# One PSUM pool for attention and experts, in a fused kernel on one Trainium2 core

## The chip, the core and the metric

The kernel runs on one core of one Trainium2 chip. The metric is the device time of one execution in microseconds (us); lower is better. A time "of the runs" is the median of several executions; the profile is of one execution more, with a time of its own.

The engines go by their profile names: PE (matrix multiply, with PEld for its weight loads), ACT, DVE and POOL for element-wise work, and SP, which here only issues transfers. PE writes its results to PSUM, an accumulator memory of eight banks; each bank holds 512 fp32 numbers on each of 128 partitions. ACT and DVE read them from there.

## The reference

Two stages. The first is a gated attention unit without a softmax, the second sends each of its 22528 output rows through a dense two-layer network and, in addition, through the one expert network (of eight) that its largest logit picks, weighted by that expert's softmax probability.

```python
# u, v: [8, 2816, 256]   z: [8, 2816, 64]   F = 512, E = 8
scores = (1.0 / S) * np.matmul(z, z.transpose(0, 2, 1))
x = (u * np.matmul(np.maximum(scores, 0.0) ** 2, v)).reshape(22528, 256)

y = np.maximum(x @ w1_dense, 0.0) @ w2_dense
e = np.argmax(x @ w_gate, axis=1)             # gate_w = softmax(x @ w_gate)[e]
y += gate_w[:, None] * (np.maximum(x @ w1[e], 0.0) @ w2[e])      # row by row
```

## The kernel before

The whole program is unrolled in Python. The order of PE, ACT, DVE and SP is the order in which the code calls them (a manual schedule); a framework then gives each tile its place and adds every semaphore wait. A tile that is taken anew from a pool waits until all users of the tile that held its place are done.

**Attention.** The loop over `groups` works a batch off in blocks of 128 queries. `scores` makes score tiles `s` on PE, `relu` turns them into the squared matrix `A` in two steps on ACT, DVE or POOL, `av` multiplies them with `v` into `o` (L603), and `gate_x` (L630) multiplies `o` by `u`, which gives two blocks of rows of `x`. `s`, `o`, and the small routing products (`lg` for the logits, `pre` for counts) all lie in four pairs of PSUM banks. A pair is asked for with `take_pair`, given back with `give_pair`, and a tile on it is made with `banks(x, name)`, which takes a new tile of the tag `b0` to `b3` from the pool `ps` (one place for each tag). Which pair is taken next follows times that the code estimates as it writes the program.

**Routing.** For each group `q` of row blocks (eleven blocks, with smaller ones at the end) `logits`, `route_a`, `route_pre` and `route_b` find each row's expert and its place in a table in DRAM, and `scatter` writes the rows there (L749). The last two groups are routed in the expert phase (`late_routing`, `late_places`), and their `lg` and `pre` tiles come from the expert phase's PSUM tiles: for the last but one from the `y` tiles, for the last from the `s` tiles (function `small`).

**Experts.** After the loop the attention's pool is closed, and two pools are opened on its banks:

```python
attention.close()
late["s"] = pool("psS", 3, space=bass.MemoryType.PSUM)     # three tiles of two banks
late["y"] = pool("psY", 2, space=bass.MemoryType.PSUM)     # two tiles of one bank
```

Then `slot(s)` is called for each tile of 256 rows, 90 of them. For tile `s` a slot makes the dense hidden layer (`up` with `w1d`), the second half of tile `s - 2`, the expert's hidden layer of tile `s` (`up` with the expert's weights), and the first half of tile `s - 1`. Between, it fetches rows some slots ahead over SP (`fetch`) and copies the weights of the next tile's expert into a ring with DVE (`expert`, L960).

- `up` writes eight matmuls into one `h_ps` tile of two banks (L973), and ACT applies Relu into the ring of hidden tiles (L976).
- `half(s, j)` does 128 rows: four matmuls for the dense part into `y[:, 0, :]`, four for the expert's into `y[:, 1, :]`, both in one `yy` tile of one bank (L982); ACT copies the dense part to SBUF (L999); DVE multiplies the expert's part by the gate and adds the copy (L1000); POOL writes the rows to the output by an indirect DMA (L1002). For some halves POOL also runs a small copy (`pause`, L987).

So PE's order in the expert phase is: 8 matmuls of `h_ps`, 8 of `yy`, 8 of `h_ps`, 8 of `yy`, and so on. The `yy` tiles alternate between the two places of `psY`, the `h_ps` tiles go round the three of `psS`.

Of the kernel before, what the change touches and what calls it, by code (L numbers as in the profile page):

```python
# [8 lines left out]
F32 = mybir.dt.float32  # L9
# [6 lines left out]
P = 128  # L16
# [3 lines left out]
def kernel(  # L20
# [13 lines left out]
    B, S, D = u.shape  # L34
# [11 lines left out]
    nQ = len(sizes)  # L46
# [21 lines left out]
    def pool(name, bufs, **kw):  # L68
        return ctx.enter_context(tc.tile_pool(name=name, bufs=bufs, **kw))
# [6 lines left out]
    tt = pool("tt", 1)  # L76
    mx = pool("mx", 6)
    NS = 4
    attention = ExitStack()
    ps = attention.enter_context(tc.tile_pool(name="ps", bufs=1, space=bass.MemoryType.PSUM))  # L80
    late = {}

    def banks(x, name, shape=(P, 2, 4 * P), dt=F32):

        return ps.tile(list(shape), dt, name=name, tag=f"b{x}")
# [61 lines left out]
    def load_u(g, gate=False):  # L147
        ut = aw.tile([P, 2, D], F32, name="ut", bufs=3)
        if gate:
            nc.vector.memset(ut[:, 0, 0:1], 0.0)  # L150
        b, i = divmod(g, nK)
        nc.sync.dma_start(out=ut[:], in_=uf[:, b, i:i + 2, :])
        issue(0.6)
        ut_of[g] = ut[:]
# [131 lines left out]
    pairs = [(0.0, x) for x in range(NS - 2)]  # L286
# [49 lines left out]
    def until(cond):  # L336

        while cond() is None:
            pick = best()
            assert pick is not None  # L340
            now[0] = max(now[0], pick[0][0])
            give(pick)
        now[0] = max(now[0], cond())
        run(now[0])
# [38 lines left out]
    def take_pair():  # L383
        return pairs.pop(0)[1]
# [82 lines left out]
    def block(n, k, c):  # L467

        w = groups[n][2]
        for a in far[n]:  # L470
            _, j0, wj = groups[a]
            if j0 <= k < j0 + wj:
                x = c * wj + k - j0
                return turned_to(a, n, w)[:, x * P:(x + 1) * P]
        return A[n][:, k, c * P:(c + 1) * P]

    def far_steps(a):

        _, j0, wj = groups[a]

        def step(ns):
            n = ns[0]
            i0, w = groups[n][1], sum(groups[m][2] for m in ns)
            if n == a + 2:
                open_group(a + 1)
                open_group(n)
            nc.sync.dma_start_transpose(
                out=turned_to(a, n, w).rearrange("p (x c) -> p x c", c=P),
                in_=A[a][:, i0:i0 + w, :].rearrange("p k c -> p (k c)"))
            issue(0.18 * w * wj, read_at.get(a - 1, 0.0) if n == a + 2 else 0.0)  # L490
            read_at[a] = sync[0] + 3.5
            for m in ns:
                for j in range(wj):
                    key_at[m, j0 + j] = sync[0] + 3.0

        ns = [[n] for n in range(a + 2, min(a + 6, len(groups))) if a in far[n]]
        if len(ns) == 4:
            ns[2:] = [ns[2] + ns[3]]
        elif groups[a][2] == 4:
            ns = ns[1:] + ns[:1]  # L500
        return [(a, lambda m=m: step(m), m[-1]) for m in ns]
# [5 lines left out]
    def fill(n, force=False):  # L507

        if jobs and jobs[0][0] <= now[0] and room(1):
            jobs.pop(0)[1]()  # L510
            return True
        m = ahead(n)
        busy = sum(1 for op in todo if op[0] in (1, 4))
        if m is not None and room(1) and busy <= (4 if n < 2 else 2):
            scores(m, left[m].pop(0))
            return True
        return False
# [9 lines left out]
    def v_at(n, k):  # L527

        return 3.3 + 2.6 * (4 * k // nK) if n == 0 else 0.0

    def need(n, k):

        while max(key_at.get((n, k), 9e9), v_at(n, k)) > now[0]:
            if fill(n):
                continue
            pick = best()
            ts = [t for t, _ in pairs if t > now[0]]
            ts += [max(key_at[n, k], v_at(n, k))] if (n, k) in key_at else []
            assert pick is not None or ts
            if pick is not None and (not ts or pick[0][0] <= min(ts)):  # L540
                now[0] = max(now[0], pick[0][0])
                give(pick)
            else:
                now[0] = min(ts)
        run(now[0])
# [31 lines left out]
    def av(n, i, between):  # L577
        b, i0, w = groups[n]
        if i == i0:
            turning.extend(far_steps(n))  # L580
        keep[0] = 0
        if n == 0 and i == i0:

            fill(n)
            need(n, 0)
        until(lambda: pairs[0][0] if pairs else None)
        ox = take_pair()
        o = banks(ox, "o")
        for p in range(2):
            rest = list(range(nK))  # L590
            for x in range(nK):
                k = rest[0]
                if i == i0 and p == 0:

                    k = min(rest, key=lambda k: (max(key_at.get((n, k), 9e9), v_at(n, k)), k))
                    need(n, k)
                rest.remove(k)
                if n == 0 and i == i0 and p == 0 and x in (12, 14, 16):
                    load_u(2 * (x - 12) // 2, gate=True)
                for h in range(2):  # L600
                    r = slice(h * dq, (h + 1) * dq)
                    j = p ^ h
                    nc.tensor.matmul(out=o[:, j, 0:D], lhsT=block(n, k, i + j - i0)[r],  # L603
                                     rhs=v_of[b][r, k, :], start=(p == 0 and x == 0),
                                     stop=(p == 1 and x == nK - 1))
                pe(0.1092)
                keep[0] = 2 - p if x >= nK - 12 else 0
                if x % 2 == 1 and x < nK - 1:
                    fill(n)
                if x in (3, 10, 17)[1 - p:] and turning and sync[0] <= now[0] + 0.5:  # L610
                    t = can_turn(turning[0][2], turning[0][0])
                    if t is not None and t <= now[0]:
                        turning.pop(0)[1]()
            if p == 0:
                swap_rows(n)
                between()

        def done(t):
            give_pair(t + 0.1, ox)

        g = b * nK + i
        offer(now[0] + 0.2, 0, {"dve": (0.63, lambda eng: gate_x(g, o))}, done)
        keep[0] = 0
# [21 lines left out]
    def small(q, name, shape):  # L645
        if q < nQ - 2:
            return banks(bank_of[q], name, shape)
        tag = "y" if q == nQ - 2 else "s"
        return late[tag].tile(list(shape), F32, name=name, tag=tag)

    def logits(q):
        n = sizes[q]
# [311 lines left out]
    def up(xT, ws):  # L964

        m = xT.shape[1]
        h_ps = late["s"].tile([P, 4, 2, P], F32, name="h_ps", tag="s")
        n = m // len(ws)
        for i, w1 in enumerate(ws):
            hs = slice(i * n, (i + 1) * n)  # L970
            for f in range(4):
                for c in range(2):
                    nc.tensor.matmul(out=h_ps[:, f, hs, :], lhsT=w1(c, f), rhs=xT[:, hs, c, :],  # L973
                                     start=(c == 0), stop=(c == 1))
        h = take("h")
        nc.scalar.activation(h[:, :, 0:m * P], h_ps[:, :, 0:m, :].rearrange("p f h t -> p f (h t)"),  # L976
                             AF.Relu)
        return h
# [12 lines left out]
    def half(s, j):  # L991

        hd, he, we, me, ids = pend[s]
        we = we[j % len(we)]
        yd, ys = take("yd"), take("ys")
        y = late["y"].tile([P, 2, D], F32, name="yy", tag="y")
        down(y, 0, hd, lambda f: w2d[:, f, :], j)
        down(y, 1, he, lambda f: we[:, 2 * F + f * D:2 * F + (f + 1) * D], j)
        nc.scalar.copy(yd, y[:, 0, :])  # L999
        nc.vector.scalar_tensor_tensor(out=ys, in0=y[:, 1, :], scalar=me[:, j, 0:1],  # L1000
                                       in1=yd, op0=ALU.mult, op1=ALU.add)
        ins = nc.gpsimd.indirect_dma_start(  # L1002
            out=out, out_offset=bass.IndirectOffsetOnAxis(ap=ids[j], axis=0),
            in_=ys, in_offset=None, bounds_check=N - 1, oob_is_err=False)
        nodep(ins, ["out"], "out")
        last_row[0] = ins
        if j == 0 and s < NT1:
            pause(ys)
# [180 lines left out]
    while jobs:  # L1189
        jobs.pop(0)[1]()  # L1190
        run(9e9)
    attention.close()
    late["s"] = pool("psS", 3, space=bass.MemoryType.PSUM)
    late["y"] = pool("psY", 2, space=bass.MemoryType.PSUM)
    for s in range(NT - MAYBE + 2):
        assert s + AHEAD < NT1 or not waiting
        slot(s, NT - MAYBE)
# [45 lines left out]
```

## Time and profile before

| what | value |
|---|---|
| median of 3 runs | 905.04 us (904.14 to 910.75) |
| profiled execution, its own time | 909.34 us |
| its span | 907.6 us |
| PE busy | 862.3 us, 95% of the span |
| ACT busy | 697.8 us, 77% |
| DVE busy | 667.2 us, 74% |
| POOL busy | 468.1 us, 52% |
| granted PE clock | 0.998 of full speed |
| first matmul into `h_ps` | 552.0 us |
| first and last matmul into `yy` | 554.8 us and 899.1 us |

In the groups of instructions, `L999 ACT COPY ring<-yy` is the ACT copy at line 999, which reads the tile `yy` and writes a tile named `ring`; then come the shapes and the count, the busy time and the mean of one in ns, and after the second bar how long the engine had been idle right before these instructions and what ended most of it. In a timeline each row has start, duration, engine, line, operation, and in brackets the idle time before it. A row of windows has a stretch, its length, and the busy time of PE, PEld, DVE, ACT and POOL with the count of instructions, then the granted PE clock, the DMA share and the rate. A row of waits has who waited for whom, the total in us, how often, and the longest. The ends of matmuls are modelled: PE starts one of the small ones every 0.109 us, and the profile gives each 0.272 us.

### The profile page before, as it was taken

The page shows a single profiled execution, that of the slowest core. Times are in us where ns is not written, and L with a number is a line of the kernel's source. Part 1 is how long each engine was busy: PE and PEld are TensorE (multiplying, and loading weights), DVE is VectorE, ACT ScalarE, POOL GpSimd, SP SyncE. Part 2 cuts the span into 40 slices and gives each one's busy share as a digit, 9 for nine tenths or more (in the row PEclk, how much of TensorE's full clock was granted, in tenths as well). Part 3 has the DMA queues.
Part 4 walks back from the last instruction along what each step waited for, and adds up shares of the span by engine and source line. Part 5 has one row for each costly group of instructions (what it writes and reads, how often), then busy time and mean ns, then how long its engine had stood idle before and what let it go on. Part 6 is the DMA issues. An engine that isn't in the chain of part 4 may idle for free.

```text
span 907.6 us, 30096 instructions
## 1 busy us (share of the span) xinstructions
PE 862.3 (95%) x12178; PEld 754.2 (83%) x12178; DVE 667.2 (74%) x1268; ACT 697.8 (77%) x871; POOL 468.1 (52%) x510
## 2 busy tenths in 40 slices
PE   7999999999999999999999999988989898999996
PEld 5898798898898888889889877877878787888885
DVE  7998898898889889889889976456644444546554
ACT  8988798888889879879879964666666666776664
POOL 8202343343353444343334354777778777877454
PEclk9999999999999999999999999999999999999999
DMA  9999999999999999999998874645434453443332
GB/s 179 156 192 165 184 193 169 201 196 180 213 182 186 199 178 187 199 175 195 205 178 153 163 126 94 129 113 116 112 101 115 108 109 107 109 103 100 88 89 83
DMA packets 288238, 136.80 MB, mean 151 GB/s; under 512 B 258526, under 2 KB 265950, under 8 KB 287200
## 3 DMA queue, kind: packets, MB, share of 16 engines
q1 hardware_dynamic: 263552, 79.40, 52.5%
q0 software_dynamic: 24544, 55.44, 26.3%
q8 instruction: 96, 1.57, 0.7%
q14 instruction: 46, 0.38, 0.1%
HBM read 61.54 MB, written 37.03 MB: 109 GB/s over the span
## 4 chain that ended last, share of the span: by engine, by line
PE 70%; POOL 10%; issue 9%; DVE 4%; ACT 3%; DMA 2%; POOLq 0%; another core or an unknown queue 0%; DVEq 0%; SPq 0%; ACTq 0%
PE o L603 41%; PE yy L982 9%; PE h_ps L973 9%; PE s L405 9%; POOL out_dram L1002 7%; POOL zr L987 1%; DMA out_dram<-ring,ix 1%; ACT A L433 1%; ACT r L420 1%; DVE r L422 1%; PE lg L659 1%; POOL A L435 1%; DMA wall<-A 1%; DVE ring L1000 1%; ACT ring L999 1%
## 5 line engine op out<-in xcount | busy, mean ns | idle before, releaser
L603 PE MATMUL o<-vb,A 64*128 64x256 bf16 x7184 | 458.9, 269 | 3.1 <-POOL A L435 1.3
L603 PEld LDWEIGHTS <-A 64*128 64x128 bf16 x7184 | 378.8, 94 | 44.2 <-issue 3.3
L749 POOL DMA_INDIRECT xs<-pays,pi x176 | 191.9, 1090 | 283.0 <-DVE pi L747 232.1
L420 ACT ACTIVATE r<-s 128x1024 f32<-128x1024 f32 (+1 forms) x252 | 247.1, 1011 | 44.4 <-PE s L405 42.1
L976 ACT ACTIVATE ring<-h_ps 128x1024 bf16<-128x1024 f32 x180 | 184.6, 1027 | 96.1 <-PE h_ps L973 61.1
L433 ACT ACTIVATE A<-r 128x1024 bf16<-128x1024 f32 (+1 forms) x238 | 242.1, 1047 | 7.3 <-DMA wall<-A 4.6
L1000 DVE SCALAR_TENSOR_TENSOR ring<-yy,me,ring 128x256 f32<-128x256 f32 x179 | 85.6, 481 | 154.3 <-ACT ring L999 82.9
L435 DVE TENSOR_TENSOR A<-r 128x1024 bf16<-128x1024 f32 x151 | 182.9, 1221 | 4.0 <-ACT r L420 3.0
L422 DVE TENSOR_SCALAR r<-s 128x1024 f32<-128x1024 f32 (+1 forms) x145 | 175.0, 1214 | 8.7 <-PE s L405 6.0
L1002 POOL DMA_INDIRECT out_dram<-ring,me x140 | 147.1, 1051 | 66.2 <-DVE ring L1000 31.2
L982 PEld LDWEIGHTS <-ring 128*128 128x128 bf16 x1432 | 138.9, 98 | 44.6 <-issue 28.9
L405 PE MATMUL s<-zT 64*128 64x512 bf16 (+1 forms) x874 | 145.1, 355 | 1.8 <-ACT zT L199 0.6
L982 PE MATMUL yy<-w2d,ring 128*128 128x256 bf16 x716 | 107.3, 272 | 22.8 <-DVE ring L1000 20.2
L982 PE MATMUL yy<-ring 128*128 128x256 bf16 x716 | 107.6, 273 | 0.3 <-issue 0.3
L973 PE MATMUL h_ps<-ring 128*128 128x256 bf16 (+1 forms) x872 | 94.6, 254 | 1.2
L973 PE MATMUL h_ps<-ring,w1d 128*128 128x256 bf16 x720 | 93.1, 272 | 2.3 <-DVE pays L630 1.6
L999 ACT COPY ring<-yy 128x256 f32<-128x256 f32 x179 | 67.7, 378 | 29.2 <-PE yy L982 18.1
L960 DVE COPY ring<-wall 128x2048 bf16 x109 | 81.8, 765 | 10.2 <-issue 6.2
L630 DVE TENSOR_TENSOR pays<-o,ut 128x512 bf16<-128x512 f32 x88 | 60.2, 685 | 30.6 <-PE o L603 29.0
L973 PEld LDWEIGHTS <-ring 128*128 128x128 bf16 x872 | 73.0, 98 | 11.7 <-DVE ring L960 2.7
L973 PEld LDWEIGHTS <-w1d 128*128 128x128 bf16 x720 | 69.9, 98 | 11.0 <-issue 3.0
L405 PEld LDWEIGHTS <-zT 64*128 64x128 bf16 x874 | 54.2, 94 | 17.5 <-issue 6.7
(122 smaller groups left out, 426.6 us busy)
## 6 DMA issues: line engine op xcount, KB each, us to landing
ut<-in_u_dram SPq DMA_DIRECT2D x88, 256.0 KB
vb<-in_v_dram POOLq DMA_DIRECT2D x7, 1408.0 KB
wall<-in_moe_w_dram POOLq DMA_DIRECT2D x16, 256.0 KB
xs<-pays,pi POOLq DMA_INDIRECT x176
zr<-in_z_dram POOLq DMA_DIRECT2D x7, 352.0 KB
out_dram<-ring,me POOLq DMA_INDIRECT x140
ring<-xs SPq DMA_TRANSPOSE x114
xT<-pays SPq DMA_TRANSPOSE x88
```

The lines of the kernel that those rows point to most:

```text
L405: nc.tensor.matmul(out=s[:, h, y * c:(y + 1) * c], lhsT=zT[r, k + h, :], rhs=zT[r, i0:i0 + w, :], start=True, stop=True)
L420: nc.scalar.activation(r[:, :, :c], s[:, :, :c], AF.Relu, scale=1.0 / S)
L422: nc.vector.tensor_scalar(out=r[:, :, :c], in0=s[:, :, :c], scalar1=1.0 / S, scalar2=0.0, op0=ALU.mult, op1=ALU.max)
L433: nc.scalar.activation(a, r, AF.Square)
L435: (nc.gpsimd if eng == "pool" else nc.vector).tensor_mul(a, r, r)
L603: nc.tensor.matmul(out=o[:, j, 0:D], lhsT=block(n, k, i + j - i0)[r], rhs=v_of[b][r, k, :], start=(p == 0 and x == 0), stop=(p == 1 and x ...
L749: ins = nc.gpsimd.indirect_dma_start(out=xs, out_offset=bass.IndirectOffsetOnAxis(ap=pi[:], axis=0), in_=pays[:, g % (2 * G), 0:ROW].bitca ...
L973: nc.tensor.matmul(out=h_ps[:, f, hs, :], lhsT=w1(c, f), rhs=xT[:, hs, c, :], start=(c == 0), stop=(c == 1))
L976: nc.scalar.activation(h[:, :, 0:m * P], h_ps[:, :, 0:m, :].rearrange("p f h t -> p f (h t)"), AF.Relu)
L982: nc.tensor.matmul(out=y[:, k, :], lhsT=h[:, f, j * P:(j + 1) * P], rhs=w2(f), start=(f == 0), stop=(f == 3))
L1000: nc.vector.scalar_tensor_tensor(out=ys, in0=y[:, 1, :], scalar=me[:, j, 0:1], in1=yd, op0=ALU.mult, op1=ALU.add)
L1002: ins = nc.gpsimd.indirect_dma_start(out=out, out_offset=bass.IndirectOffsetOnAxis(ap=ids[j], axis=0), in_=ys, in_offset=None, bounds_chec ...
```

## The change

The pool `ps` stays open for the whole kernel, and the pools `psS` and `psY` are gone. After the attention loop, the pair that was not used by the last `o` and is first free becomes one tile named `yy`; its two banks serve the halves in turn, as slices `yy[:, 0, :]` and `yy[:, 1, :]`. The two other such pairs and then the pair of the last `o` serve `h_ps` in turn; for each `h_ps` a new tile is taken with `banks`. The `lg` and `pre` of the last but one group are slices of the `yy` tile, those of the last group new tiles on the `h_ps` pairs. No instruction is added or taken out on any engine.

```diff
     NS = 4
-    attention = ExitStack()
-    ps = attention.enter_context(tc.tile_pool(name="ps", bufs=1, space=bass.MemoryType.PSUM))
+    ps = pool("ps", 1, space=bass.MemoryType.PSUM)
+    last_o = []
...
         ox = take_pair()
         o = banks(ox, "o")
+        last_o[:] = [ox]
...
     def small(q, name, shape):
         if q < nQ - 2:
             return banks(bank_of[q], name, shape)
-        tag = "y" if q == nQ - 2 else "s"
-        return late[tag].tile(list(shape), F32, name=name, tag=tag)
+        if q == nQ - 1:
+            return next_h(name, shape)
+        a, b = shape[1:]
+        return next_y()[:, 0:a * b].rearrange("p (a b) -> p a b", b=b)
+
+    def next_h(name, shape):
+        late["h"].append(late["h"].pop(0))
+        return banks(late["h"][-1], name, shape)
+
+    def next_y():
+        late["y"].append(late["y"].pop(0))
+        return late["y"][-1]
...
-        h_ps = late["s"].tile([P, 4, 2, P], F32, name="h_ps", tag="s")
+        h_ps = next_h("h_ps", (P, 4, 2, P))
...
-        y = late["y"].tile([P, 2, D], F32, name="yy", tag="y")
+        y = next_y().rearrange("p (k d) -> p k d", d=D)
...
-    attention.close()
-    late["s"] = pool("psS", 3, space=bass.MemoryType.PSUM)
-    late["y"] = pool("psY", 2, space=bass.MemoryType.PSUM)
+    other = [x for _, x in pairs if x not in last_o]
+    assert len(other) == NS - 1
+    yy = banks(other.pop(0), "yy")
+    late["y"] = [yy[:, x, :] for x in range(2)]
+    late["h"] = other + last_o
```

## The prediction

> **What bounds the kernel now.** I read the page's head first, then the groups of the expert phase, one stretch of windows over that phase, the waits, and three pieces of the timeline: a quiet piece, a stall, and the change of phase.
>
> ```profile
> span 907.6 us, 30096 instructions
> PE 862.3 (95%) x12178; PEld 754.2 (83%) x12178; DVE 667.2 (74%) x1268; ACT 697.8 (77%) x871; POOL 468.1 (52%) x510
> PE 70%; POOL 10%; issue 9%; DVE 4%; ACT 3%; DMA 2%; POOLq 0%; another core or an unknown queue 0%; DVEq 0%; SPq 0%; ACTq 0%
> L999 ACT COPY ring<-yy 128x256 f32<-128x256 f32 x179 | 67.7, 378 | 29.2 <-PE yy L982 18.1
> L1000 DVE SCALAR_TENSOR_TENSOR ring<-yy,me,ring 128x256 f32<-128x256 f32 x179 | 85.6, 481 | 154.3 <-ACT ring L999 82.9
> ...
> L982 PE MATMUL yy<-w2d,ring x716: 269/272/273, 554.8 to 898.7; 128*128 128x256 bf16 x179
> ...
> 559.20:894.00 334.80, 309.80 (x2917) 270.42 (x2916) 173.85 (x366) 220.77 (x346) 240.87 (x277) 1.00 0.46 106
> ...
> PE yy L982 <- DVE ring L1000: 20.2, 22, 2.4
> ```
>
> PE is the bound, and the chain that ended last runs over PE for 70% of the span. The expert phase runs from the first yy matmul at 554.8 to the last at 898.7 and a few microseconds more. There are 716/4 = 179 "halves" of 128 tokens in it. In each, PE makes 8 matmuls into h_ps and 8 into one yy tile; ACT copies the dense part of yy (L999, 378 ns); DVE combines the two parts (L1000, 481 ns). PE is busy 309.8 of 334.8 us between 559.2 and 894.0, so there is little idle time for a new wait to hide in. PE already waits for the combining, 20.2 us in all, but only 22 times in 179: with two yy tiles it waits for the half before the last.
>
> The quiet piece is the one to learn from:
>
> ```profile
> 700.22 0.60 PE L982 MATMUL yy<-w2d,ring 128*128 128x256 bf16 x4
> 700.65 0.60 PE L982 MATMUL yy<-ring 128*128 128x256 bf16 x4
> 701.09 1.04 PE L973 MATMUL h_ps<-ring 128*128 128x256 bf16 x8
> 701.34 0.37 ACT L999 COPY ring<-yy 128x256 f32<-128x256 f32 x1
> 701.79 0.48 DVE L1000 SCALAR_TENSOR_TENSOR ring<-yy,me,ring 128x256 f32<-128x256 f32 x1 [1.26 <-issue]
> 701.96 0.60 PE L982 MATMUL yy<-w2d,ring 128*128 128x256 bf16 x4
> 702.16 1.02 ACT L976 ACTIVATE ring<-h_ps 128x1024 bf16<-128x1024 f32 x1 [0.46 <-issue]
> 702.50 0.73 DVE L960 COPY ring<-wall 128x2048 bf16 x1 [0.22 <-issue]
> 703.21 0.37 ACT L999 COPY ring<-yy 128x256 f32<-128x256 f32 x1
> 703.62 0.48 DVE L1000 SCALAR_TENSOR_TENSOR ring<-yy,me,ring 128x256 f32<-128x256 f32 x1 [0.39 <-ACT ring L999]
> 703.71 0.60 PE L982 MATMUL yy<-w2d,ring 128*128 128x256 bf16 x4
> ```
>
> The halves start at 700.22, 701.96 and 703.71: 1.745 us apart, PE without a gap. The half of 700.22 leaves PE at 701.25, is copied by 701.71 and combined by 702.27. That is 0.31 us after the next half has begun (701.96). The next one is combined at 704.10, 0.39 us after its successor began. So here PE always begins a half before the one ahead of it is combined. It may do so because there are two yy tiles.
>
> **The change part by part.** The tiles keep their places and sizes: three pairs of banks for h_ps, two banks for yy. No instruction is added on any engine, and the order on each is the same; two things move.
>
> First, the two yy tiles, which a pool gave out anew for each half, are now two slices of one long-lived tile. In the program as built this shows in the semaphore each first yy matmul waits for. Before, it waits for the DVE count that the combining two halves back sets; after, for the count of the combining just ahead of it, although that one reads the other bank. (At one place in mid-phase the count goes from 1027 to 1029; 1027 is the combining from the half before the last, 1029 that from the last.) A wait that PE formerly had on the copied expert weights drops out, because the later count covers it. So what is written as two buffers waits like one.
>
> Here a rule of the Trainium skill speaks the other way. PSUM — Partial Sum Buffer, section "PSUM bank collisions raise a hardware error", says that engines need to be kept apart by bank and quadrant, and that accesses to different banks run clean. By that rule alone the wait is needless and the time would be the third rival's; the rows of before do not show a wait between slices of one tile, so the trace is silent, and the built program's counts decide.
>
> The price of one half then is a closed loop: yy matmuls, copy, combining, next yy. From the rows above: 700.22 to 701.25 (matmuls, 1.03), to the copy 0.09, copy 0.37, to the combining 0.08, combining 0.48; and 0.05 from there to PE, which is what lies between the combining's end at 590.39 and PE's start at 590.44 in the stall below. Sum 2.10; where ACT's end releases DVE at once (703.58 to 703.62, 0.04) it is 2.06. I take 2.09 against 1.745. The 8 h_ps matmuls, 0.87 us, run inside the loop. What could stretch it has room. ACT's Relu of h_ps now ends before the copy: its matmuls begin right behind the yy ones, 0.87 after those began, and end 1.04 later, the Relu starts some 0.08 after and takes 1.02, so it is through at 3.01, and the next copy is due at 2.09 + 1.03 + 0.09 = 3.21. DVE's weight copy (0.73, begun 0.23 after a combining) is through about 1 us after that combining; the next is due 1.6 us after it. Behind the waiting PE stand only the h_ps matmuls of the next tile, which feed ACT later and nobody sooner.
>
> From the half at 559.21 to that at 893.99 there are 172 such loops: 172 x (2.09 - 1.745) = **+59 us**.
>
> The stalls: these 172 cycles took 334.8 us and not 172 x 1.745 = 300.1, so 34.7 us are lost to something else. One case:
>
> ```profile
> 586.23 0.60 PE L982 MATMUL yy<-w2d,ring 128*128 128x256 bf16 x4
> 587.97 0.60 PE L982 MATMUL yy<-w2d,ring 128*128 128x256 bf16 x4
> 589.50 0.37 ACT L999 COPY ring<-yy 128x256 f32<-128x256 f32 x1 [1.40 <-PE yy L982]
> 589.91 0.48 DVE L1000 SCALAR_TENSOR_TENSOR ring<-yy,me,ring 128x256 f32<-128x256 f32 x1 [2.59 <-ACT ring L999]
> 590.44 0.60 PE L982 MATMUL yy<-w2d,ring 128*128 128x256 bf16 x4 [0.56 <-issue]
> 592.51 0.37 ACT L999 COPY ring<-yy 128x256 f32<-128x256 f32 x1 [0.49 <-PE h_ps L973]
> 593.51 0.60 PE L982 MATMUL yy<-w2d,ring 128*128 128x256 bf16 x4 [1.16 <-DVE ring L1000]
> 595.25 0.60 PE L982 MATMUL yy<-w2d,ring 128*128 128x256 bf16 x4
> ```
>
> The half of 586.23 should have been through PE at 587.26, yet ACT, idle, begins its copy at 589.50: for some microseconds PE's completions reach ACT late. PE loses (590.44 - 587.97 - 1.745) + (593.51 - 590.44 - 1.745) = 2.05 us; the slack of a second tile swallowed the rest. About 34.7/2.05 = 17 such cases would make the whole. I cannot say what makes them late. For the forecast I leave their cost as it is (0). Bounds: they vanish when PE no longer runs without a pause, **-35**; or the slack that is gone makes each dearer. In the case shown, PE would begin at 590.44 what it began at 587.97, and the next at about 593.5: two loops in 7.2 us where 4.18 are due, 3.0 lost and not 2.05, times 17: **+17**.
>
> The second move is the change of phase:
>
> ```profile
> 550.26 0.10 PEld L973 LDWEIGHTS <-w1d 128*128 128x128 bf16 x1 [0.21 <-issue]
> 551.98 1.03 PE L973 MATMUL h_ps<-ring,w1d 128*128 128x256 bf16 x8 [1.64 <-DVE pays L630]
> 556.31 0.48 DVE L1000 SCALAR_TENSOR_TENSOR ring<-yy,me,ring 128x256 f32<-128x256 f32 x1
> 557.47 0.60 PE L982 MATMUL yy<-w2d,ring 128*128 128x256 bf16 x4
> 558.56 0.19 DVE L726 TENSOR_TENSOR inc<-inc,pre 128x32 f32<-128x32 f32 x1
> 559.21 0.60 PE L982 MATMUL yy<-w2d,ring 128*128 128x256 bf16 x4
> ```
>
> The first h_ps no longer waits for the last gating (L630), 1.64 us; its pair has been free for long. But the late routing's small products now lie in the same yy tile. The second yy (557.47) must wait for the DVE step that ends at 558.75, 1.96 us after the first combining's end (556.79), and the third for the second's combining. The first combining may come 1 to 1.5 us earlier, at 555.3 to 555.8, so the second yy starts at 557.3 to 557.8 and the third 2.09 later, at 559.4 to 559.9 and not 559.21. The gain is spent within three halves: I take **0** (bounds -1.6 and +0.7).
>
> The end:
>
> ```profile
> 893.99 0.60 PE L982 MATMUL yy<-w2d,ring 128*128 128x256 bf16 x4
> 894.86 0.60 PE L982 MATMUL yy<-w2d,ring 128*128 128x256 bf16 x4
> 898.38 0.60 PE L982 MATMUL yy<-w2d,ring 128*128 128x256 bf16 x4
> 900.73 0.48 DVE L1000 SCALAR_TENSOR_TENSOR ring<-yy,me,ring 128x256 f32<-128x256 f32 x1 [1.05 <-ACT ring L999]
> ```
>
> The last five halves have less or no h_ps work between them, and take 901.21 - 893.99 = 7.2 us to the last combining. As closed loops they take 5 x 2.09 - 0.05 = 10.4: **+3.2**. What follows, the last writes, moves along.
>
> The sum is 59 + 3 + 0 = +62 us. The profiled execution took 909.3 us (span 907.6); the median of the runs is 905.0, 4.3 lower, and I put the sum on the median: **967 us**.
>
> **The rivals.** *Stalls vanish:* if late completions come only from PE running flat out, 967 - 35 = 932. For it: the quiet piece has none, so they are no fixed tax on each half; against: PE will still issue 16 matmuls at the same pace in each loop. *Stalls grow:* 967 + 17 = 984. For it: there is no slack left, and DVE's lateness goes straight into PE. *The change does what it says:* the wait between the two slices doesn't bind, the loops stay at 1.745, and only the first wait goes: 905.0 - 1.6 = 903.4, no slower than before. It would take the waits in the built program not to be those I read; the loop decides as soon as a half's combining ends later than the next start, which the quiet piece shows for each half.
>
> **How the numbers follow.** Forecast 0.43, stalls grow 0.30, stalls vanish 0.22, the change does what it says 0.05. The range 930 to 994 takes in the first three, with 10 us above the dearest for what a slower phase may add to the stalls in number; it leaves out the last. A measurement of this kernel can tell about 1% (9 us) from no change. The first three are all slower by more; the last is within 1% but for a small part: faster 0.01, same 0.04, slower 0.95.
>
> **What would show it.** In the changed profile the yy matmuls should start about 2.09 us apart in quiet pieces, each 0.05 us behind a combining's end; the waits should have "PE yy on DVE ring" some 170 times and not 22, with 60 us or more; PE's busy share of the expert phase should fall from 0.93 to about 0.8; everything before 550 us should be unchanged, and the first h_ps should start about 1.6 us earlier. Starts still 1.745 apart would refute the whole. Starts at 2.09 with a time under 940 or over 980 would refute only the term of the stalls.

## The result, and the profile after

The changed kernel takes 940.94 us (median of 6 runs, 939.36 to 944.34) against 906.32 us of the kernel before (6 runs, 904.14 to 911.93). The ratio is 1.0377 with a 95% interval of 1.0338 to 1.0417: **34.6 us slower**. The profiled execution of the changed kernel took 941.09 us, with a span of 939.4; that of before had a span of 907.6. So the two traces are 31.8 us apart, and this is the difference that is laid out below.

The changed kernel's page and groups, then the same stretch of windows as before, from the third yy half to the last but four, and the waits:

```profile
span 939.4 us, 30096 instructions
PE 883.6 (94%) x12178; PEld 755.9 (80%) x12178; DVE 664.4 (71%) x1268; ACT 716.6 (76%) x871; POOL 472.6 (50%) x510
...
L993 PE MATMUL yy<-w2d,ring x716: 269/271/273, 555.4 to 933.3; 128*128 128x256 bf16 x179
```

```profile
561.70:924.90 363.20, 328.51 (x2915) 271.21 (x2915) 170.23 (x364) 239.26 (x346) 244.97 (x277) 1.00 0.42 99
```

```profile
PEld L993 <- issue: 67.5, 176, 1.6
...
PE yy L993 <- DVE ring L1011: 26.2, 79, 1.4
```

The same 172 cycles that took 334.8 us take 363.2, with the same work in them: 28.4 of the 31.8 us lie here. (The lines have moved: L984 is the matmul into h_ps, L987 its Relu, L993 the yy matmul, L1010 ACT's copy, L1011 DVE's combining, L1013 the output write.) A piece of the timeline at the place where the prediction's quiet piece lay shows what they have become:

```profile
700.59 0.60 PE L993 MATMUL yy<-w2d,ring 128*128 128x256 bf16 x4
701.02 0.60 PE L993 MATMUL yy<-ring 128*128 128x256 bf16 x4
701.46 1.04 PE L984 MATMUL h_ps<-ring 128*128 128x256 bf16 x8
701.66 0.37 ACT L1010 COPY ring<-yy 128x256 f32<-128x256 f32 x1
702.12 0.48 DVE L1011 SCALAR_TENSOR_TENSOR ring<-yy,me,ring 128x256 f32<-128x256 f32 x1 [1.52 <-issue]
702.53 1.02 ACT L987 ACTIVATE ring<-h_ps 128x1024 bf16<-128x1024 f32 x1 [0.50 <-PE h_ps L984]
702.66 0.60 PE L993 MATMUL yy<-w2d,ring 128*128 128x256 bf16 x4 [0.16 <-DVE ring L1011]
703.73 0.37 ACT L1010 COPY ring<-yy 128x256 f32<-128x256 f32 x1 [0.17 <-PE yy L993]
704.14 0.48 DVE L1011 SCALAR_TENSOR_TENSOR ring<-yy,me,ring 128x256 f32<-128x256 f32 x1 [0.59 <-ACT ring L1010]
704.67 0.60 PE L993 MATMUL yy<-w2d,ring 128*128 128x256 bf16 x4
```

The halves start at 700.59, 702.66 and 704.67, 2.07 and 2.01 us apart, where they were 1.745 apart. The combining that begins at 702.12 ends at 702.60, and the next half starts at 702.66; the one of 704.14 ends at 704.62, and the next starts at 704.67. In the timeline of the whole stretch the start follows the end of the combining just ahead of it by 0.05 to 0.06 us in 177 of 178 pairs; the exception is the first pair, at the change of phase, which is taken up below. That is the closed loop of the prediction.

One more number matters for what follows. Call a copy *late* when ACT begins it more than 0.5 us after the modelled end of its half's matmuls. Counted over the traces, before has 81 late copies in 179 halves, the worst 4.06 us; after has 11, the worst 1.28. In 64 of the 81 ACT sits idle for a part of that time; in the other 17 it is still busy with the Relu ahead. Since the ends of matmuls are modelled, a late copy does not tell whether the matmul itself ended late or its signal came late.

### The profile page after: what moved, and what is told of

It reads as the page before. It is cut to its first block, busy times and chain, and to the rows that moved or that the text cites. A ratio compares the mean times of both kernels' runs of the same rounds, so it can differ in the third digit from the quotient of the medians.

```text
span 939.4 us, 30096 instructions
## 1 busy us (share of the span) xinstructions
PE 883.6 (94%) x12178; PEld 755.9 (80%) x12178; DVE 664.4 (71%) x1268; ACT 716.6 (76%) x871; POOL 472.6 (50%) x510
## 5 line engine op out<-in xcount | busy, mean ns | idle before, releaser
L760 POOL DMA_INDIRECT xs<-pays,pi x176 | 196.6, 1117 | 284.2 <-DVE pi L758 234.0
L987 ACT ACTIVATE ring<-h_ps 128x1024 bf16<-128x1024 f32 x180 | 183.4, 1020 | 93.6 <-PE h_ps L984 77.8
L1011 DVE SCALAR_TENSOR_TENSOR ring<-yy,me,ring 128x256 f32<-128x256 f32 x179 | 86.4, 483 | 185.4 <-ACT ring L1010 73.2
L993 PEld LDWEIGHTS <-ring 128*128 128x128 bf16 x1432 | 138.9, 97 | 82.2 <-issue 67.5
L1013 POOL DMA_INDIRECT out_dram<-ring,me x140 | 154.6, 1104 | 83.3 <-DVE ring L1011 54.4
L993 PE MATMUL yy<-w2d,ring 128*128 128x256 bf16 x716 | 106.9, 271 | 37.9 <-DVE ring L1011 26.2
L993 PE MATMUL yy<-ring 128*128 128x256 bf16 x716 | 107.4, 273 | 0.0
L1010 ACT COPY ring<-yy 128x256 f32<-128x256 f32 x179 | 66.7, 373 | 45.8 <-PE yy L993 28.0
L984 PE MATMUL h_ps<-ring,w1d 128*128 128x256 bf16 x720 | 92.9, 272 | 1.9 <-DMA ring<-xs 1.9
L984 PE MATMUL h_ps<-ring 128*128 128x256 bf16 (+1 forms) x872 | 93.3, 253 | 0.0
L971 DVE COPY ring<-wall 128x2048 bf16 x109 | 76.7, 719 | 16.9 <-issue 10.4
L984 PEld LDWEIGHTS <-ring 128*128 128x128 bf16 x872 | 73.9, 98 | 6.8
L984 PEld LDWEIGHTS <-w1d 128*128 128x128 bf16 x720 | 69.8, 98 | 10.3 <-DMA ring<-xs 2.1
```

Source lines behind the costliest of these rows:

```text
L760: ins = nc.gpsimd.indirect_dma_start(out=xs, out_offset=bass.IndirectOffsetOnAxis(ap=pi[:], axis=0), in_=pays[:, g % (2 * G), 0:ROW].bitca ...
L993: nc.tensor.matmul(out=y[:, k, :], lhsT=h[:, f, j * P:(j + 1) * P], rhs=w2(f), start=(f == 0), stop=(f == 3))
L1013: ins = nc.gpsimd.indirect_dma_start(out=out, out_offset=bass.IndirectOffsetOnAxis(ap=ids[j], axis=0), in_=ys, in_offset=None, bounds_chec ...
```

## The experiments

All were timed beside the kernel before on the same chip. The chips differ in time, so each time is read against the "before" given with it. "First chip" is the chip of the first eight experiments, whose "before" of 906.07 us is close to the 906.32 of the result; two other chips follow.

**1. The two yy places as two tiles.** The changed kernel, with its one pool, but each half takes a new yy tile on one of two pairs of banks in turn; h_ps goes round the two other pairs.

```diff
-    def next_y():
+    def next_y(name, shape):
         late["y"].append(late["y"].pop(0))
-        return late["y"][-1]
+        return banks(late["y"][-1], name, shape)
...
-        y = next_y().rearrange("p (k d) -> p k d", d=D)
+        y = next_y("yy", (P, 2, D))
...
-    yy = banks(other.pop(0), "yy")
-    late["y"] = [yy[:, x, :] for x in range(2)]
-    late["h"] = other + last_o
+    late["y"] = [other[0], other[2]]
+    late["h"] = [other[1]] + last_o
```

> The pool stays one and open; yy is a new tile for each half, on two pairs of banks in turn, and h_ps goes round the two other pairs and not three. If the cost is that two slices of one tile wait like one buffer, starts of yy are 1.745 us apart again in quiet pieces and the time is that of before, 903 to 910 us. If the cost lies in the one open pool or in the moved banks, it stays near 941. If h_ps needs its third pair, the starts are apart by more than 1.745 and PE waits for ACT's Relu.

Measured: 908.26 us against 906.07, ratio 1.0008 (0.9983 to 1.0033). Groups and waits of this kernel:

```profile
L992 PE MATMUL yy<-w2d,ring x716: 269/272/417, 552.5 to 900.5; 128*128 128x256 bf16 x179
...
PE yy L992 <- DVE ring L1010: 4.7, 13, 0.6
```

The halves start 1.747 us apart again, and the waits for the combining are 13 and not 79. So the single pool costs nothing that can be seen, and neither does h_ps on two pairs. What costs is that the two places are one tile.

**2. The kernel before with one yy buffer.**

```diff
-    late["y"] = pool("psY", 2, space=bass.MemoryType.PSUM)
+    late["y"] = pool("psY", 1, space=bass.MemoryType.PSUM)
```

> The kernel before with its two pools, but one yy tile and not two; nothing else is moved. If one buffer for yy is the whole cost of the change, it is as slow as the change: 938 to 944 us, starts 2.04 us apart. If the open pool or the moved banks have a share in the 35 us, it comes out well under 935.

Measured: 941.26 us against 906.07, ratio 1.0401 (1.0343 to 1.0459). Groups and waits:

```profile
L982 PE MATMUL yy<-w2d,ring x716: 269/271/273, 552.9 to 930.7; 128*128 128x256 bf16 x179
...
PEld L982 <- issue: 68.8, 177, 1.4
...
PE yy L982 <- DVE ring L1000: 27.2, 84, 1.3
```

One buffer in one bank gives the whole loss, the same pair of intervals (2.01 and 2.07), the same waits and the same 11 late copies as the change with its two banks. The second bank of the change buys no time. Here the rule of the Trainium skill that the prediction weighed (PSUM — Partial Sum Buffer, section "PSUM bank collisions raise a hardware error") can be placed: accesses to different banks may well run clean, but this wait doesn't come from the banks. The changed kernel has two banks and waits, experiment 1 has two tiles and does not. The measurement decides, as the built program's counts had it.

**3. The quick first h_ps without the loop.** Three of the pairs stay open for the whole kernel, the fourth has its own pool, which is closed and opened as `psY` with two tiles. The cuts of the code stand against the kernel before.

```diff
-    ps = attention.enter_context(tc.tile_pool(name="ps", bufs=1, space=bass.MemoryType.PSUM))
+    ps = pool("ps", 1, space=bass.MemoryType.PSUM)
+    ps3 = attention.enter_context(tc.tile_pool(name="ps3", bufs=1, space=bass.MemoryType.PSUM))
...
     attention.close()
-    late["s"] = pool("psS", 3, space=bass.MemoryType.PSUM)
     late["y"] = pool("psY", 2, space=bass.MemoryType.PSUM)
+    late["h"] = other + last_o
```

> Three pairs serve both phases in one open pool, as in the change; only the fourth pair's pool is closed, and two real yy tiles are opened in its place. By the loop of one buffer the time is that of before or 1 to 2 us less, since the first h_ps does not wait for the last gating: 902 to 907 us. If taking h_ps anew on the attention's pairs costs something in itself, it is slower than before.

Measured: 907.6 us against 906.07, ratio 1.0012 (0.9982 to 1.0042), no gain that can be seen. Its yy group:

```profile
L990 PE MATMUL yy<-w2d,ring x716: 269/272/417, 552.1 to 894.2; 128*128 128x256 bf16 x179
```

The yy matmuls begin 2.7 us earlier than before (552.1 against 554.8), but the median of the runs shows none of it. Nor need the open pool be what brings the early start: experiment 2, which closes the pool as before, begins at 552.9. With 1 and 2 this settles the mechanism: the open pool is worth nothing either way, and the single tile is the whole of the loss.

**4. The pace without the wait.** The first three experiments left a question of size: the loop should have cost over 50 us, and 35 were measured. Before, with two tiles, gets three more matmuls at the head of each half, which the following start=True discards. PE then needs as long for a half as the loop does, but never has to wait.

```diff
     def down(y, k, h, w2, j):
+        for _ in range(3 if k == 0 else 0):
+            nc.tensor.matmul(out=y[:, k, :], lhsT=h[:, 0, j * P:(j + 1) * P],
+                             rhs=w2(0), start=True, stop=True)
```

> The kernel before, with three more matmuls in each half (the first dense one is repeated), so that PE needs 1.745 + 3 x 0.109 = 2.07 us for a half, the pace of the change, but without a wait in each. If the late completions come from PE running on without a pause, they stay: 906 + 58 = 964 us or more. If they come from a pace of 1.745 that ACT, DVE, POOL or the transfers cannot follow, they go, as in the change: 930 to 942 us.

Measured: 932.54 us against 906.07, ratio 1.0293 (1.0243 to 1.0344). That is 26.5 us for 3 x 179 matmuls, which at 0.109 us each are 58.5 us of PE. Group, and a row of windows from the middle of the phase:

```profile
L985 PE MATMUL yy<-w2d,ring x716: 272/273/273, 552.4 to 921.1; 128*128 128x256 bf16 x179
```

```profile
660.00:800.00 140.00, 140.00 (x1285) 125.45 (x1283) 59.83 (x111) 91.62 (x136) 103.41 (x123) 1.00 0.41 103
```

PE is busy for 140.00 of 140 us and starts a half every 2.074 us, with a mean over the phase of 2.079. So at this pace the stalls cost almost nothing, though PE never pauses. The late copies haven't all gone: 33 are left, up to 2.0 us. But with two tiles a half may run late by two intervals less one loop before PE has to wait, which is 2 x 2.074 - 2.04 = 2.1 us here and 2 x 1.745 - 2.04 = 1.45 in before (an estimate from the intervals and the loop measured above), and fewer copies are late besides, 33 and not 81. "PE pauses, and so completions come in time" is not needed for the cost to go; the slower pace alone gives back some 32 us. A part for the pauses is not excluded: at nearly the same pace the change has 11 late copies and this kernel 33.

**5. A third of that.** The same edit with `range(1 ...)`, one more matmul.

> The kernel before with one more matmul in each half: PE needs 1.745 + 0.109 = 1.855 us for a half, still less than the 1.93 us that a half takes on average before. If the 35 us of stalls are a fixed cost for each event, the time rises by 178 x 0.109 = 19 us to 925. If they are what is left of an average pace that something other than PE sets, the time stays at 905 to 910 and PE's stalls shrink to about 15 us.

Measured: 920.55 us against 915.34 in the same minutes, ratio 1.0078 (1.0052 to 1.0104). That is 5 us in place of 179 x 0.109 = 19.5. The group of this kernel:

```profile
L985 PE MATMUL yy<-w2d,ring x716: 270/273/421, 558.0 to 912.0; 128*128 128x256 bf16 x179
```

Starts in quiet pieces are 1.856 apart, the mean is 2.00: 0.14 us a half, or 25 us, are still lost to stalls. At 1.747 the trace of experiment 7, timed beside this one, loses (1.981 - 1.747) x 172 = 40 us, and that of before lost 35. The cost falls with the pace by degrees.

**6. A pause for PE in one half of four.** Before, with two yy places of one tile each, and every fourth half put on the place just used.

```diff
+    made = [0, 0]
+
+    def y_tag():
+        made[0] += 1
+        if made[0] % 4:
+            made[1] ^= 1
+        return f"y{made[1]}"
...
-        y = late["y"].tile([P, 2, D], F32, name="yy", tag="y")
+        y = late["y"].tile([P, 2, D], F32, name="yy", tag=y_tag())
...
-    late["y"] = pool("psY", 2, space=bass.MemoryType.PSUM)
+    late["y"] = pool("psY", 1, space=bass.MemoryType.PSUM)
```

> The kernel before with its two yy tiles, but one half in four takes the place of the half just ahead of it, and so waits for its combining as in the change: 44 waits of about 0.3 us. If late completions build up while PE runs on without a pause, these pauses cut them and it is faster than before, 885 to 900 us. If something else sets the average pace, the pauses fall into time that is lost anyway: 904 to 912 us. If the costs add up: 906 + 13 = 919 us.

Measured: 930.07 us against 915.34, ratio 1.016 (1.0116 to 1.0205), so 14.7 us. The waits:

```profile
PEld L984 <- issue: 50.7, 49, 3.4
...
PE yy L984 <- DVE ring L1009: 28.8, 26, 3.1
```

44 single loops at 0.295 us are 13 us, so the time shows the loops and nothing given back. The trace (of the slowest of the four runs, 937.98 us) has a mean of 2.037 us a half, where 1.747 and the loops alone would make 1.82, and 56 late copies. A pause in one half of four does not take the cost of the stalls away.

**7. No small copies on POOL.** `pause` returns at once; the copies feed no output.

```diff
     def pause(src):
-        nc.gpsimd.tensor_copy(take("idle")[:, :src.shape[1]], src)
+        return
```

> The kernel before without POOL's small copies (L987), whose results nobody reads; POOL then issues its transfers with nothing between. If POOL's load sets the average pace of 1.93 us, it is faster: by up to the 35 us of stalls, 875 to 900 us. If POOL's load has no part in the stalls: 904 to 908 us. If its transfers then crowd each other or the fetches, slower than 908.

Measured: 915.35 us against 915.34, ratio 1.0013 (0.9983 to 1.0043). The waits:

```profile
ACT ring L976 <- PE yy L982: 41.7, 29, 3.0
...
PE yy L982 <- DVE ring L1000: 27.3, 27, 2.0
```

109 copies are late now, in 44 runs of one or more halves (before has 30 such runs), and the time is the same. POOL's copies are not needed for the stalls, and leaving them out is no cure.

**8. The late scatters at each slot, not at each third.**

```diff
-        if s % 3 == 1 and waiting:
+        if s >= 1 and waiting:
```

> The kernel before, with the scatters of the late routing in each slot from the second on and not in each third; they are through by about 625 us and not by 775. If a scatter is what makes PE's completions late, the stalls crowd before 625 and are gone from 630 to 775, where before lost about 15 us: 890 to 900 us. If the stalls have nothing to do with the scatters, they stay where they were: 904 to 908 us.

Measured: 911.94 us against 915.34, ratio 0.9983 (0.9952 to 1.0015). The total hardly moves, but look at where it is lost. Three windows of this kernel, then the same three of before:

```profile
560.00:660.00 100.00, 77.24 (x655) 64.45 (x653) 45.44 (x116) 52.69 (x81) 77.85 (x97) 0.97 0.48 105
660.00:800.00 140.00, 140.00 (x1283) 125.45 (x1282) 69.80 (x136) 103.41 (x160) 106.81 (x121) 1.00 0.53 114
800.00:890.00 90.00, 88.51 (x928) 78.77 (x926) 51.75 (x108) 62.88 (x99) 57.27 (x58) 1.00 0.39 97
```

```profile
560.00:660.00 100.00, 90.96 (x824) 79.48 (x822) 56.05 (x134) 65.16 (x103) 76.02 (x90) 1.00 0.54 116
660.00:800.00 140.00, 127.56 (x1148) 111.66 (x1147) 62.17 (x117) 92.62 (x144) 108.18 (x130) 1.00 0.46 108
800.00:890.00 90.00, 86.97 (x908) 76.01 (x906) 52.29 (x106) 59.49 (x95) 55.25 (x57) 1.00 0.38 96
```

While the crowded scatters run (the last starts at 651 us, in before at 775), PE loses 22.8 of 100 us, 9.0 in before. Once they are through, it is busy for 140.00 of 140 us at starts of 1.747, where before still loses 12.4. (The trace of before is from another time; in experiment 7, taken beside this one, PE is busy for 87.68 and 124.93 us in these windows, so there too the stalls go on past 660.) So on this chip a good part of the stalls moves with the scatters of the late routing. But the scatters are not all of it: from 840 us on this kernel loses some 4 us again, though its last scatter is long over, and before loses some 9 us behind its own last one (both counted from the starts of the halves); 31 of the 53 late copies here, and 31 of the 81 there, come after the last scatter. The clock that PE was granted is not what differs: it is 1.00 in the first two windows of before, where PE loses 9.0 and 12.4 us.

**9 and 10. Fewer output writes, on a second chip.** Before and after, each with the output write left out for the second half of every tile; so those 128 rows of each tile stay unwritten in these two.

```diff
+        if j == 1:
+            return
         ins = nc.gpsimd.indirect_dma_start(
```

> The kernel before, with the output's second halves left unwritten: POOL issues no write for them, so its indirect transfers stand 3.5 us apart and not 1.75, or nearer where a scatter comes in between; the matmuls, copies and combinings are all there. If PE's completions are late because POOL's indirect transfers follow each other too closely, the stalls go, and with them about 30 us: 870 to 885 us. If POOL has no part in them: 900 to 910 us.

> The same cut in the changed kernel (the output's second halves are left unwritten). Its loop of 2.04 us stays, and only the 12 us of stalls that it still has can go: 925 to 935 us. Its distance from the kernel before with the same cut is then the price of the loop alone, 178 x (2.04 - 1.745) = 52 us. If the stalls of before and the loop have nothing to do with each other, the distance is that of the full kernels, 35 us.

This chip did not ask the question that was put to it. The kernel before, unaltered, takes 874.55 us here. Without half its writes it takes 875.22, ratio 1.0013 (0.9986 to 1.004); changed and without half its writes, 928.87, ratio to before 1.0605 (1.0573 to 1.0637). The first, then the second:

```profile
span 874.8 us, 29751 instructions
...
L982 PE MATMUL yy<-w2d,ring x716: 272/273/273, 553.1 to 865.2; 128*128 128x256 bf16 x179
```

```profile
span 929.1 us, 29751 instructions
...
L993 PE MATMUL yy<-w2d,ring x716: 269/271/273, 553.0 to 922.0; 128*128 128x256 bf16 x179
```

Neither has one late copy. The mean cycle, over the same 172 halves as above, is 1.750 us in the first and 2.056 in the second. So nothing is learned of what writes do to the stalls, since there are none to remove. But the loop is seen here alone: 928.87 - 875.22 = 53.7 us, where 172 x (2.056 - 1.750) is 52.6.

**11. More POOL copies, on the second chip.** Experiment 3 with the small POOL copy in every slot.

```diff
-        if j == 0 and s < NT1:
+        if j == 0:
             pause(ys)
```

> The kernel with the split pool (two real yy tiles), and POOL's small copy between its two writes also in the last 20 slots, which had none. If the copy spaces POOL's transfers and so keeps PE's completions on time, the 4 to 7 us of stalls of the last 35 halves shrink: 899 to 904 us, against 906 before. If it only adds to POOL's load: 906 or more.

Measured: 876.22 us against 874.55, ratio 1.0018 (1.0001 to 1.0035). The windows:

```profile
561.70:862.80 301.10, 301.10 (x2915) 271.62 (x2913) 175.46 (x363) 221.55 (x346) 252.77 (x292) 1.00 0.53 117
```

PE is busy for all of 301.10 us, so there was nothing to gain. From 560 us to the end 129 of 196 intervals between the starts of POOL's indirect transfers are under 1.6 us, and yet no copy is late: close transfers on POOL are by themselves not enough.

**12. The change again, on a third chip.** No edit.

> The change as it is, once more, beside the kernel before on whichever chip is given. The loop's own price is 178 x 0.295 = 52 us; what the change really costs is that, less the stalls which its slower pace saves. On a chip where before runs without stalls (about 875 us), all of it should show: 925 to 932 us. On one where before takes 906 us: 941 again. Where before takes more than that, the distance should be smaller than 35 us. If the price of the change does not depend on the stalls of before, the distance is 35 us on any chip.

Measured: 930.25 us (929.72 to 931.58) against 875.35 (870.86 to 877.69), ratio 1.0637 (1.0609 to 1.0666): 54.9 us. The page and the waits:

```profile
span 928.5 us, 30096 instructions
...
L993 PE MATMUL yy<-w2d,ring x716: 269/271/273, 553.0 to 922.1; 128*128 128x256 bf16 x179
...
PEld L993 <- issue: 58.8, 176, 1.2
...
PE yy L993 <- DVE ring L1011: 19.7, 86, 1.0
```

No copy is late here, and the mean cycle is 2.061. The change costs its whole loop here: 172 x (2.061 - 1.750), with the 1.750 of experiment 9, is 53.5 us. That before has no stalls to give back on this chip is inferred from its time, which is that of the second chip; no trace of it was taken here.

## Why the prediction was right in kind and 26 us off

It said 967 us, and 940.9 were measured, inside the range and on the right side. Its steps, against the two first traces:

- **Two slices of one tile wait like one buffer: right, and shown** by experiments 1 to 3 together.
- **The loop, +59: +51.** The starts alternate between 2.01 and 2.07, mean 2.04, and 2.09 had been taken. The 0.09 us from the modelled end of the matmuls to ACT's copy is 0.04 in the piece above (700.59 + 1.03 = 701.62, copy at 701.66). 172 x (2.04 - 1.745) = 51. A few loops are longer, 2.2 us and more, without any late copy: on the two other chips the mean loop is 2.056 and 2.061. By 2.06 the loops are 54 us, and the next term -26; the sum stays.
- **The stalls, 0: -23. This is the term that was mis-sized.** The 172 cycles take 363.2 us, of which 172 x 2.04 = 351 are loop; 12 us of stalls are left of 34.7. The forecast kept their cost as it was, on the thought that PE would still issue its matmuls at the same pace within each loop. The bound "they vanish" was near the truth, but its reason, that PE would pause, was not it: in experiment 4 PE never pauses and the cost goes all the same, in experiment 6 it pauses in one half of four and the cost stays. What counts in these runs is how long a half takes: 35 us lost at 1.745, 25 at 1.856, next to none at 2.07. So the measured time lies nearer to the rival "stalls vanish" (932) than to the forecast, and only 0.9 us above the 940 under which the prediction would have called this term refuted; so small a margin does not speak for the term.
- **The other bound, +17, was wrong in its premise.** It took the number of cases as fixed, at 17, and only made each dearer. But the late copies became fewer, 11 and not 81.
- **The change of phase, 0: about +1.** The first of its two events came as predicted, the second for another reason:

```profile
551.61 1.05 PE L984 MATMUL h_ps<-ring,w1d 128*128 128x256 bf16 x8
...
554.56 1.05 PE L984 MATMUL h_ps<-ring,w1d 128*128 128x256 bf16 x8 [0.84 <-DMA ring<-xs]
...
558.76 1.05 PE L984 MATMUL h_ps<-ring,w1d 128*128 128x256 bf16 x8 [1.07 <-DMA ring<-xs]
...
559.21 0.19 DVE L737 TENSOR_TENSOR inc<-inc,yy 128x32 f32<-128x32 f32 x1
...
559.65 0.60 PE L993 MATMUL yy<-w2d,ring 128*128 128x256 bf16 x4
...
561.71 0.60 PE L993 MATMUL yy<-w2d,ring 128*128 128x256 bf16 x4
```

The first h_ps starts without a wait. The attention ended 1.4 us later in this execution (DVE's last step on `inc` in it at 549.99, before at 548.64), so the start is 0.4 us and not 1.6 earlier by the clock. The second yy (559.65) does start behind the routing step, which ends at 559.40, but 0.25 us behind it. What it follows without a gap is the eight h_ps matmuls begun at 558.76, which take PE 0.87 us. What was not seen is that the h_ps tiles, being earlier, would wait for their rows, 0.84 and 1.07 us. The third half starts at 561.71 and before at 559.21: 2.5 later, less the 1.4 that came from the attention, is 1.1, somewhat above the bound of +0.7.

- **The end, +3.2: +0.9.** The last five starts run from 924.89 to 932.94, 8.05 us and not 4.39, so the loops cost 3.7. But the span ends 6.4 us after the last yy start, not 9.2 as in before. The prediction let the last writes "move along". In before they don't hang on the last combining: the last five halves start 1.1 us apart on average, POOL's last six writes 1.28 us apart, the last of them 5.4 us after the last yy start. In the changed kernel the writes keep up with the slower halves, and the last starts 2.2 us after it. (Before has a late copy there too, but that is not needed for it: in experiment 11, without one late copy and with more copies on POOL, the span ends 9.4 us after the last yy start.) The rows are the last of the changed kernel, then POOL's last writes in before and its last write in the changed kernel:

```profile
924.89 0.60 PE L993 MATMUL yy<-w2d,ring 128*128 128x256 bf16 x4
...
932.94 0.60 PE L993 MATMUL yy<-w2d,ring 128*128 128x256 bf16 x4 [0.98 <-DVE ring L1011]
...
934.42 0.48 DVE L1011 SCALAR_TENSOR_TENSOR ring<-yy,me,ring 128x256 f32<-128x256 f32 x1 [1.53 <-ACT ring L1010]
```

```profile
901.21 0.97 POOL L1002 DMA_INDIRECT out_dram<-ring,ix  x1 [0.30 <-issue]
902.49 0.97 POOL L1002 DMA_INDIRECT out_dram<-ring,ix  x1 [0.31 <-issue]
903.76 0.97 POOL L1002 DMA_INDIRECT out_dram<-ring,ix  x1 [0.30 <-issue]
```

```profile
935.18 0.97 POOL L1013 DMA_INDIRECT out_dram<-ring,ix  x1 [1.04 <-DVE ring L1011]
```

The sum of what was found, with the 1.4 us from the attention counted in the 2.5, is 51 - 22.6 + 2.5 + 0.9 = 31.8, the distance of the spans.

Of the signs, the starts and the 0.05 us behind the combining held, and between 400 and 500 us PE is busy for 99.72 us in both. Two failed, in ways that mislead. **PE's busy share did not fall to 0.8**: it is 328.5/363.2 = 0.90 where it was 0.93, and PE's busy time over the kernel rose from 862.3 to 883.6 us with the same 12178 matmuls. Each matmul is given 0.27 us though the next begins after 0.109, so the last one of a row covers half of the 0.3 us gap behind it. The weight loads show the gap better: 270.4/334.8 = 0.81 before, 271.2/363.2 = 0.75 after. **The waits were not booked where they were looked for**: "PE yy on DVE ring" has 79 and not 170, with 26.2 us, while PEld shows 67.5 us in 176 waits on the yy line, put down to "issue". There the closed loop is counted, once for nearly each of the 179 halves.

**What stays open** is what makes PE's completions reach ACT late on the first chip. The runs say that a part of it moves with the late scatters while another comes after them (8), that it costs less at a slower pace (4, 5), and that it isn't cured by pauses of PE in one half of four (6) or by leaving out POOL's copies (7). On the second chip two kernels at the pace of before have no late copy (9, 11), and close POOL transfers don't bring any about there (11); on the third the change has none (12). The test that was meant for the output writes met a chip without stalls and remains undecided. No version here is measurably faster than the kernel before.

## What to carry to other kernels

For the framework that places the waits here, two slices of one long-lived tile are one buffer; if two halves are to be in flight, they must be two tiles. Ask what a wait that is added will slow down besides itself: here the slower pace gave back about 23 of the 35 us that the kernel had been losing elsewhere, so the 51 us of the loop showed only in part. A stall of unknown cause therefore deserves a weight in the forecast near its "gone" bound when the change slows its surroundings. Measure a closed loop by the distance of its starts in the timeline, and not by PE's busy share or by the wait that one expects to be named.

## What the runs showed of the chip that was not expected

- The same program takes 906 to 915 us on one chip and 874.55 and 875.35 us on two others. As far as there are traces, the difference is the stalls: the mean cycle is 1.95 us in the trace of before (334.8/172) and 1.750 without them on the second chip in experiment 9, and 172 times the difference is 34 us. The change therefore costs 3.8% in one place and 6.4% in the other.
- On the first chip the same kernel went from 906.07 to 915.34 us within minutes, with no edit; only runs made beside each other can be compared. Where the 9 us lie is open, since no trace of the unaltered kernel was taken at the later time.
- Three more matmuls for each half, 58.5 us of PE's time, cost 26.5 us, and one more, 19.5 us, cost 5.
